# Moving three linear forms of an exponential from VectorE to GpSimd, and converting 67 packs of scores instead of 54

## The chip, the cores and the metric

The kernel runs on one core of one Trainium2 chip. The metric is the device time of one execution in microseconds (us); each version was run several times, and the medians are given. In the first set of runs one execution of the kernel before took 3240 us; it is left out of the ratios, as the fast runs alone count.

The engines are PE (matrix multiply; PEld are its weight loads), DVE (vector), ACT (activation functions), POOL (GpSimd) and SP (here only DMA). The kernel gives each its own stream of instructions in a fixed order, and lets them wait for one another by semaphores. In this kernel the tiles that are named ps_ lie in the memory PSUM, and all of PE's matmuls in the profiles write to them; the others, but for those with dram in their name, lie in the memory SBUF.

## The reference, cut to what matters

Two attention branches over the same input are mixed by a gate. Branch A is ordinary softmax attention with 32 heads of 16 dimensions over 2048 positions, and its exponentials are the bulk of the work:

```python
scores = jnp.einsum("bhqd,bhkd->bhqk", q, k) * (Dh ** -0.5)
p = _softmax(scores, axis=-1)
o = jnp.einsum("bhqk,bhkd->bhqd", p, v)
# ... branch B: linear attention with softmax features (phi); out = g * a + (1 - g) * b
```

## The kernel before

The work of branch A is cut into 32 steps `n` (a quarter of the queries times four heads), each with 16 key blocks `kt` of four score tiles of 128x512. ACT takes the exponential of most tiles, two or three at a time, from a ring of five PSUM banks. Some key blocks per step, called packs here, are taken from ACT: DVE computes their exponential by arithmetic on the bits. A multiplication and addition turn a score into an integer whose high half is the bf16 exponential with a linear mantissa and whose low half is the fraction f; a cubic correction in f is then added. `DVE_COUNT` says how many packs each step has, 54 in all.

```python
DVE_COUNT = (1, 2, 1, 1, 1, 2, 1, 2, ...)           # 54 in all
def dve_pack(self, n, kt, first_pv):
    ...
    for i in range(4):                               # four score tiles of the pack
        m = s.op("pe", ..., matmul(self.bk(b), kT, qT))
        ws.append(s.op("dve", 0.72, EW = tensor_scalar(psum, EC, 127 * 65536, mult, add)))   # int32
    f  = s.op("dve", 1.25, Ef = lo(EW) * 2**-16)     # the low halves as a fraction, f16, 128x2048
    m1 = s.op("dve", 0.71, Em = Ef - 1)
    t  = s.op("dve", 0.71, Et = Ef * (128*EB) + 128*(EA - EB/2))
    u  = s.op("dve", 1.25, Em = Ef * Em)
    g_ = s.op("dve", 1.25, Et = Et * Em)
    for hf in range(2):
        vs.append(s.op("dve", 1.23, ED = EW * 2**-9 + Et))     # uint16 = the bits of bf16
    return s.op("pe", 0.32, four matmuls: ps_ot += Vaug * ED)  # waits for vs
```

The instruction order is not written by hand. A small list scheduler in the kernel is given a planned duration for each operation (the numbers above, in us), priorities and buffer pools; it lays out each engine's program order, and the chip then runs those orders with semaphores. So a duration that is planned too short doesn't make a result wrong. It makes one engine stand, in its order, at something that is not ready, with everything behind it standing too.

The softmax here doesn't subtract the row's maximum and nothing guards it: scores larger than these inputs give would overflow.

## Time and profile before

| | before |
|---|---|
| median time (3 runs; 929.0 with a fourth) | 929.3 us |
| ACT busy | 874.7 us, 94% |
| DVE busy | 753.6 us, 81% |
| PE busy | 785.5 us, 85% |
| POOL busy | 6.6 us, 1% |

The page's first part gives each engine's busy time, share of the span and number of instructions; its second the busy tenths in 40 slices; its fourth the chain of work that ended last.

```profile
span 928.5 us, 12587 instructions
...
PE 785.5 (85%) x5227; PEld 238.8 (26%) x5227; DVE 753.6 (81%) x1062; ACT 874.7 (94%) x801; POOL 6.6 (1%) x10
...
ACT  5998999999999999999999999999999998999995
...
ACT 63%; PE 32%; DVE 2%; SPq 1%; issue 1%; DMA 0%; ACTq 0%
...
```

ACT is at 9 tenths in nearly all slices, and 63% of the chain is ACT's own work, nearly all the rest PE's. In the groups of instructions below, ps_ring is the ring of scores that ACT reads, ps_mp holds the scores of the packs and other products, and ps_ot the sums over the exponentials. A line gives: line, engine, operation, output and inputs, shape, count, busy us and mean ns, and the idle time before them with what ended it.

```profile
...
L590 ACT ACTIVATE ET<-ps_ring 128x1536 bf16<-128x1536 f32 x366 | 533.1, 1457 | 32.2 <-PE ps_ring L574 24.8 <-PE ps_ot L611 5.4
L590 ACT ACTIVATE ET<-ps_ring 128x1024 bf16<-128x1024 f32 x367 | 376.9, 1027 | 3.0 <-PE ps_ring L574 2.5 <-PE ps_ot L611 0.2
...
L645 DVE TENSOR_SCALAR EW<-ps_mp 128x512 int32<-128x512 f32 x216 | 143.4, 681 | 59.7 <-PE ps_mp L641 58.7
L660 DVE SCALAR_TENSOR_TENSOR ED<-EW,Et 128x1024 uint16<-128x1024 int32 x108 | 129.8, 1204 | 0.1
...
L655 DVE TENSOR_TENSOR Em<-Ef,Em 128x2048 f16<-128x2048 f16 x54 | 65.6, 1215 | 0.0
L650 DVE TENSOR_SCALAR Ef<-EW 128x2048 f16<-128x2048 uint16 x54 | 65.5, 1214 | 1.1
L656 DVE TENSOR_TENSOR Et<-Et,Em 128x2048 f16<-128x2048 f16 x54 | 65.3, 1209 | 0.2
...
L796 DVE TENSOR_TENSOR phi<-phi,frec 128x1024 bf16<-128x1024 bf16 x32 | 38.8, 1211 | 0.1
...
L653 DVE TENSOR_SCALAR Et<-Ef 128x2048 f16<-128x2048 f16 x54 | 36.9, 684 | 0.0
...
L668 PE MATMUL ps_ot<-ED,Vaug 128*17 128x512 bf16 x216 | 22.5, 407 | 0.3 <-DVE ED L660 0.3
...
L684 DVE TENSOR_TENSOR T_81<-T_79,rinv 128x256 bf16<-128x256 f32 x32 | 13.2, 413 | 0.1
...
```

A pack costs DVE 4 x 0.68 + 1.21 + 2 x 0.68 + 2 x 1.21 + 2 x 1.20 = 10.1 us. The last line but one (L668) is the matmul that uses a finished pack: PE waited 0.3 us for it in the whole run, so packs were never late. ACT's idle time before its exponentials (32.2 + 3.0 us) is small.

### The profile page before, as it was taken

How to read it: one execution, taken by the hardware profiler on the slowest of the kernel's cores; microseconds unless marked ns; L12 is line 12 of the kernel's file. 1: busy time of each engine (PE TensorE's matmuls, PEld its weight loads, DVE VectorE, ACT ScalarE, POOL GpSimd, SP SyncE). 2: the span in 40 equal slices, each digit the busy share in tenths (PEclk: the TensorE clock that was granted, in tenths of full speed). 3: DMA queues.
4: the chain of work that ended last, by engine and by line, in shares of the span. 5: the costliest groups of instructions: out<-in, count | busy, mean ns of one | idle time of the engine just before them, and what ended most of it. 6: DMA issues, size and time to landing. Idle time of an engine off the chain costs nothing.

```text
span 928.5 us, 12587 instructions
## 1 busy us (share of the span) xinstructions
PE 785.5 (85%) x5227; PEld 238.8 (26%) x5227; DVE 753.6 (81%) x1062; ACT 874.7 (94%) x801; POOL 6.6 (1%) x10
## 2 busy tenths in 40 slices
PE   7989998888888878888888889888787979878795
PEld 2223322222222212222222222222222223222221
DVE  3887787888986887888978786898879798899895
ACT  5998999999999999999999999999999998999995
POOL 2000000000000000000000000000000000000000
PEclk9999999999999999899999999999999799999997
DMA  5131000000000000000000000000000000000000
GB/s 109 52 73 47 1 6 3 1 4 4 4 2 3 4 4 4 4 7 4 9 10 10 4 6 9 9 7 7 1 4 4 4 4 24 4 4 4 4 1 23
DMA packets 25112, 11.18 MB, mean 12 GB/s; under 512 B 18016, under 2 KB 25056, under 8 KB 25056
## 3 DMA queue, kind: packets, MB, share of 16 engines
q1 hardware_dynamic: 23472, 9.99, 4.1%
q8 instruction: 41, 0.67, 0.3%
q10 hardware_dynamic: 1584, 0.39, 0.2%
q14 instruction: 15, 0.12, 0.0%
HBM read 3.16 MB, written 2.10 MB: 6 GB/s over the span
## 4 chain that ended last, share of the span: by engine, by line
ACT 63%; PE 32%; DVE 2%; SPq 1%; issue 1%; DMA 0%; ACTq 0%
ACT ET L590 60%; PE ps_ring L574 15%; PE ps_mp L462 6%; PE ps_ot L611 5%; PE ps_mp L869 3%; ACT phi L790 3%; PE ps_mp L641 2%; SPq L402 1%; DVE EW L645 1%; PE ps_ot L668 1%; PE ps_mp L844 0%; PE ps_mp L809 0%; DMA xT<-in_A_x_dram 0%; DVE fsum L794 0%; DMA out_dram<-outt 0%
## 5 line engine op out<-in xcount | busy, mean ns | idle before, releaser
L590 ACT ACTIVATE ET<-ps_ring 128x1536 bf16<-128x1536 f32 (+1 forms) x733 | 844.7, 1242 | 35.2 <-PE ps_ring L574 27.3
L574 PE MATMUL ps_ring<-qT,kT 64*128 64x512 bf16 (+1 forms) x1832 | 415.8, 399 | 123.6 <-ACT ET L590 118.9
L574 PEld LDWEIGHTS ps_ring<-qT,kT 64*128 64x128 bf16 (+1 forms) x1832 | 105.7, 94 | 426.5 <-ACT ET L590 289.3
L645 DVE TENSOR_SCALAR EW<-ps_mp 128x512 int32<-128x512 f32 x216 | 143.4, 681 | 59.7 <-PE ps_mp L641 58.7
L611 PE MATMUL ps_ot<-ET,Vaug 128*17 128x512 bf16 x1832 | 183.1, 395 | 2.4 <-DVE T_79 L679 1.2
L660 DVE SCALAR_TENSOR_TENSOR ED<-EW,Et 128x1024 uint16<-128x1024 int32 x108 | 129.8, 1204 | 0.1
L641 PE MATMUL ps_mp<-qT,kT 128*128 128x512 bf16 x216 | 81.0, 394 | 3.4 <-DVE EW L645 2.1
L611 PEld LDWEIGHTS ps_ot<-ET,Vaug 128*17 128x17 bf16 x1832 | 43.5, 87 | 109.0 <-issue 100.6
L650 DVE TENSOR_SCALAR Ef<-EW 128x2048 f16<-128x2048 uint16 x54 | 65.5, 1214 | 1.1
L655 DVE TENSOR_TENSOR Em<-Ef,Em 128x2048 f16<-128x2048 f16 x54 | 65.6, 1215 | 0.0
L656 DVE TENSOR_TENSOR Et<-Et,Em 128x2048 f16<-128x2048 f16 x54 | 65.3, 1209 | 0.2
L794 DVE TENSOR_REDUCE fsum<-phi 128x64 f32<-128x1024 bf16 x32 | 38.8, 1213 | 8.5 <-ACT phi L790 8.5
L462 PE MATMUL ps_mp<-xT,WA 128*128 128x512 bf16 x128 | 38.2, 392 | 1.5 <-DMA xT<-in_A_x_dram 1.5
L796 DVE TENSOR_TENSOR phi<-phi,frec 128x1024 bf16<-128x1024 bf16 x32 | 38.8, 1211 | 0.1
L462 PE MATMUL ps_mp<-Wp,xT 128*128 128x512 bf16 x128 | 38.4, 383 | 0.3 <-DVE EW L645 0.3
L652 DVE TENSOR_SCALAR Em<-Ef 128x2048 f16<-128x2048 f16 x54 | 36.7, 680 | 0.7
L653 DVE TENSOR_SCALAR Et<-Ef 128x2048 f16<-128x2048 f16 x54 | 36.9, 684 | 0.0
L679 DVE STREAM_TRANSPOSE T_79<-ps_ot 128x512 f32<-128x512 f32 x32 | 22.9, 715 | 17.2 <-PE ps_ot L611 17.2
L790 ACT ACTIVATE phi<-ps_mp 128x512 bf16<-128x512 f32 x64 | 34.9, 604 | 0.9 <-PE ps_mp L462 0.9
L641 PEld LDWEIGHTS ps_mp<-qT,kT 128*128 128x128 bf16 x216 | 19.7, 97 | 39.5 <-issue 18.3
L519 DVE CAST Vaug<-ps_mp 128x128 bf16<-128x128 f32 (+1 forms) x32 | 13.3, 424 | 13.3 <-PE ps_mp L462 13.2
L869 PE MATMUL ps_mp<-WoA,onT_A 128*128 128x512 bf16 x64 | 20.0, 395 | 3.9 <-DVE onT_A L692 2.3
(66 smaller groups left out, 377.7 us busy)
## 6 DMA issues: line engine op xcount, KB each, us to landing
out_dram<-outt SPq DMA_DIRECT2D x16, 128.0 KB, 1.7
qT<-qst SPq DMA_DIRECT2D x120, 16.0 KB, 1.8
WA<-in_A_wqkv_dram SPq DMA_DIRECT2D x3, 384.0 KB, 4.2
WBV<-in_B_wqkv_dram SPq DMA_DIRECT2D x1, 512.0 KB, 4.5
WoA<-in_A_wo_dram SPq DMA_DIRECT2D x1, 512.0 KB, 3.8
WoB<-in_B_wo_dram SPq DMA_DIRECT2D x1, 512.0 KB, 4.5
WA<-in_A_wqkv_dram ACTq DMA_DIRECT2D x3, 128.0 KB, 3.2
xT<-in_A_x_dram SPq DMA_TRANSPOSE x16, 2.7
```

The lines of the kernel that those rows point to most:

```text
L462: m = s.op("pe", self.c_mm(n), lambda e, c=c: e.matmul(self.bk(b)[:, 0:n], lhs(c), rhs(c), start=(c == 0), stop=(c == 3)), deps if c == 0 ...
L574: return lambda e: e.matmul(self.ps_ring[:, x % RING, :], self.kT[r, g // 2, kt * P:(kt + 1) * P], self.qT[r, n % 2, i, :], start=True, st ...
L590: self.o_exp.append(s.op("act", w * 0.427 + 0.09, lambda e, b0=b0, s0=s0, w=w: e.activation(self.ET[:, s0:s0 + w, :], self.ps_ring[:, b0:b ...
L611: return lambda e: e.matmul(self.ps_ot[32 * i:32 * i + VSL, :], self.Vaug[:, kt, h, :], self.ET[:, (4 * p + k) % NSLOT, :], start=(kt == 0 ...
L641: m = s.op("pe", self.c_mm(512), lambda e, i=i, b=b: e.matmul(self.bk(b), self.kT[:, cp, kt * P:(kt + 1) * P], self.qT[:, n % 2, i, :], st ...
L645: ws.append(s.op("dve", 0.72, lambda e, i=i, b=b: e.tensor_scalar(self.EW[:, ew.idx, i * QCH:(i + 1) * QCH], self.bk(b), float(EC), float( ...
L650: f = s.op("dve", 1.25, lambda e: e.tensor_scalar(self.Ef[:], lo(), float(2.0 ** -16), None, op0=ALU.mult), ws + [self.ed_prev], pr)
L655: u = s.op("dve", 1.25, lambda e: e.tensor_tensor(self.Em[:], self.Ef[:], self.Em[:], ALU.mult), [m1], pr)
L656: g_ = s.op("dve", 1.25, lambda e: e.tensor_tensor(self.Et[:], self.Et[:], self.Em[:], ALU.mult), [t, u], pr)
L660: vs.append(s.op("dve", 1.23, lambda e, c0=c0: e.scalar_tensor_tensor(out=self.ED[:, ed.idx, c0], in0=self.EW[:, ew.idx, c0], scalar=float ...
L790: ex.append(s.op("act", 0.53, lambda e, sg=sg: e.activation(self.phi[:, ph.idx, :, sg, :], self.bk(b).rearrange("p (h f) -> p h f", f=DH), ...
L869: m = s.op("pe", self.c_mm(512), lambda e, src=src, pr=pr, W=W, k=k: e.matmul(self.bk(b), src(), W[:, pr, :], start=(k == 0), stop=(k == l ...
```

## The change

It moves the three linear forms of f (Ef, Em and what was Et) to POOL as multiply-adds straight from the low halves of EW, in halves of 1024 elements. That leaves four big operations of a pack on DVE besides the conversions, and the room is used for more packs. The announcement says 66; the counts add up to 67. Buffers are cut to make space, the copies of K, Q and V get an earlier priority, and the output matmuls wait for all their inputs at the first. A few planned durations of unchanged operations are altered as well (the conversion from 0.72 to 0.67 us, for example).

```diff
-DVE_COUNT = (1, 2, 1, 1, 1, 2, 1, 2, ... 2, 1, 2, 3, 2, 2)
+DVE_COUNT = (1, 2, 2, 2, 2, 2, 2, 2, ... 2, 2, 3, 3, 3, 3)
@@ buffers
-        Ef, Em, Et single; ED 2 buffers; T1, rinv 2; outt 3; phi 6; VB 6
+        Ef, Em 2 buffers; Eg 3 (takes Et's and ED's place); T1, rinv 1; outt 2; phi 5; VB 5
@@ priorities of the copies of Q, K, V: deadline dl
-                         dl - 4 if n0 else dl)
+                         dl - 24 if n0 else dl)
...
@@ dve_pack
-        f = s.op("dve", 1.25, ... tensor_scalar(self.Ef[:], lo(), float(2.0 ** -16), None, op0=ALU.mult), ...)
-        m1 = s.op("dve", 0.71, ... Em = Ef - 1 ...)
-        t = s.op("dve", 0.71, ... Et = Ef * 128*EB + ... )
+        for hf in range(2):
+            c0 = slice(hf * 2 * QCH, (hf + 1) * 2 * QCH)
+            for dst, a1, a0 in forms:                       # Ef, Em, Eg
+                fr.append(s.op("pool", 1.15, lambda e, ...: e.tensor_scalar(
+                    dst()[:, c0], self.EW[:, ew.idx, c0].bitcast(dt.uint16)...[:, :, 0], a1, a0,
+                    op0=ALU.mult, op1=ALU.add), ws[2 * hf:2 * hf + 2], pr))
         u:  Em = Ef * Em      (now waits for the six forms)
         g_: Eg = Eg * Em
         vs: Eg (uint16) = EW * 2**-9 + Eg, in place, two halves
```

More of the change, by code (lines that the diff above doesn't have):

```diff
@@ L32 @@
 EA, EB = 0.34370964, 0.07826797
-DVE_COUNT = (1, 2, 1, 1, 1, 2, 1, 2, 2, 1, 2, 2, 1, 2, 2, 2, 1, 2, 2, 1, 2, 2, 2, 1, 2, 2, 2, 1, 2, 3, 2, 2)
+DVE_COUNT = (1, 2, 2, 2, 2, 2, 2, 2, 2, 2, 2, 2, 2, 2, 2, 2, 2, 2, 2, 2, 2, 2, 2, 2, 2, 2, 2, 2, 3, 3, 3, 3)
 def dve_tiles(n):
@@ L328, in memory @@
         self.EW_p = BufPool(2)
-        at("Ef", [P, 4 * QCH], dt.float16)
-        at("Em", [P, 4 * QCH], dt.float16)
-        at("Et", [P, 4 * QCH], dt.float16)
-        at("ED", [P, 2, 4 * QCH], dt.uint16)
-        self.ED_p = BufPool(2)
-        at("T1", [P, 2, 16, 32], f32)
-        at("rinv", [P, 2, 16], f32)
+        at("Ef", [P, 2, 4 * QCH], dt.float16)
+        at("Em", [P, 2, 4 * QCH], dt.float16)
+        at("Eg", [P, 3, 4 * QCH], dt.float16)
+        self.Eg_p = BufPool(3)
+        at("T1", [P, 16, 32], f32)
+        at("rinv", [P, 16], f32)
         at("T2", [P, 16, 32], bf)
         self.oacc = nc.alloc_sbuf_tensor_at("oacc", [P, 4, D], f32, offset=self.wbt_off)
-        at("outt", [P, 3, D], bf)
-        self.outt_p = BufPool(3)
-        at("phi", [P, 6, H, 2, DH], bf)
-        self.phi_p = BufPool(6)
-        at("VB", [P, 6, 8, 65], bf)
-        self.VB_p = BufPool(6)
+        at("outt", [P, 2, D], bf)
+        self.outt_p = BufPool(2)
+        at("phi", [P, 5, H, 2, DH], bf)
+        self.phi_p = BufPool(5)
+        at("VB", [P, 5, 8, 65], bf)
+        self.VB_p = BufPool(5)
         at("fsum", [P, 2, 64], f32)
@@ L509, in emit_kT @@
         self.o_kT[(cp, j)] = self.evac(b, m, lambda e: e.tensor_copy(
-            self.kT[:, cp, j * QCH:(j + 1) * QCH], self.bk(b)), 512, dl)
+            self.kT[:, cp, j * QCH:(j + 1) * QCH], self.bk(b)), 512, dl - 20 if cp else dl)
     def emit_V(self, t, part):
@@ L520, in emit_V @@
             self.Vaug[:, t, h0:h0 + nh, 0:DH], self.bk(b)[:, 0:n].rearrange("p (h d) -> p h d", d=DH)),
-            n, dl, [self.o_vones])
+            n, dl - 20 if part else dl, [self.o_vones])
     def main_chain(self):
@@ L533, in main_chain @@
             pos.append(pos[-1] + 64 - 4 * len(dve_tiles(n)))
-        self.ed_prev = None
+        self.eq_prev = self.ml_prev = None
         self.units = units
@@ L635, in dve_pack @@
         pr = rel + 12
-        ew, ed = Buf(self.EW_p, 2), Buf(self.ED_p, 1)
+        ew, eg = Buf(self.EW_p, 2), Buf(self.Eg_p, 1)
         ws = []
-        m = None
+        m = self.eq_prev
         for i in range(4):
@@ L642, in dve_pack @@
                 self.bk(b), self.kT[:, cp, kt * P:(kt + 1) * P], self.qT[:, n % 2, i, :], start=True, stop=True),
-                self.o_qT[n] + [self.o_kT[(cp, kt // 4)]], pr, rel, alloc=[b, ew] if i == 0 else [b], cols=512,
+                self.o_qT[n] + [self.o_kT[(cp, kt // 4)]], pr, rel, alloc=[b, ew, eg] if i == 0 else [b], cols=512,
                 order=[m])
-            ws.append(s.op("dve", 0.72, lambda e, i=i, b=b: e.tensor_scalar(
+            ws.append(s.op("dve", 0.67, lambda e, i=i, b=b: e.tensor_scalar(
@@ L646, in dve_pack @@
                 self.EW[:, ew.idx, i * QCH:(i + 1) * QCH], self.bk(b), float(EC), float(127 * 65536),
                 op0=ALU.mult, op1=ALU.add), [m], pr, frees=[b]))
-            self.qk_dve[n] = m
-        lo = lambda: self.EW[:, ew.idx, :].bitcast(dt.uint16).rearrange("p (n two) -> p n two", two=2)[:, :, 0]
-        f = s.op("dve", 1.25, lambda e: e.tensor_scalar(self.Ef[:], lo(), float(2.0 ** -16), None, op0=ALU.mult),
-                 ws + [self.ed_prev], pr)
-        m1 = s.op("dve", 0.71, lambda e: e.tensor_scalar(self.Em[:], self.Ef[:], 1.0, None, op0=ALU.subtract), [f], pr)
@@ L653, in dve_pack @@
-        t = s.op("dve", 0.71, lambda e: e.tensor_scalar(
-            self.Et[:], self.Ef[:], float(128 * EB), float(128 * (EA - EB / 2)), op0=ALU.mult, op1=ALU.add), [f], pr)
-        u = s.op("dve", 1.25, lambda e: e.tensor_tensor(self.Em[:], self.Ef[:], self.Em[:], ALU.mult), [m1], pr)
-        g_ = s.op("dve", 1.25, lambda e: e.tensor_tensor(self.Et[:], self.Et[:], self.Em[:], ALU.mult), [t, u], pr)
+            self.qk_dve[n] = self.eq_prev = m
+        scale = float(2.0 ** -16)
+        forms = ((lambda: self.Ef[:, ew.idx], scale, 0.0), (lambda: self.Em[:, ew.idx], scale, -1.0),
+                 (lambda: self.Eg[:, eg.idx], float(128 * EB) * scale, float(128 * (EA - EB / 2))))
@@ new lines, in dve_pack @@
+        fr = []
+        for hf in range(2):
+            c0 = slice(hf * 2 * QCH, (hf + 1) * 2 * QCH)
+            for dst, a1, a0 in forms:
+                fr.append(s.op("pool", 1.15, lambda e, c0=c0, dst=dst, a1=a1, a0=a0: e.tensor_scalar(
+                    dst()[:, c0], self.EW[:, ew.idx, c0].bitcast(dt.uint16).rearrange(
+                        "p (n two) -> p n two", two=2)[:, :, 0], a1, a0, op0=ALU.mult, op1=ALU.add),
+                    ws[2 * hf:2 * hf + 2], pr))
+        u = s.op("dve", 1.25, lambda e: e.tensor_tensor(
+            self.Em[:, ew.idx], self.Ef[:, ew.idx], self.Em[:, ew.idx], ALU.mult), fr, pr)
@@ L657, in dve_pack @@
+        g_ = s.op("dve", 1.25, lambda e: e.tensor_tensor(
+            self.Eg[:, eg.idx], self.Eg[:, eg.idx], self.Em[:, ew.idx], ALU.mult), [u], pr)
         vs = []
@@ L659, in dve_pack @@
             c0 = slice(hf * 2 * QCH, (hf + 1) * 2 * QCH)
-            vs.append(s.op("dve", 1.23, lambda e, c0=c0: e.scalar_tensor_tensor(
-                out=self.ED[:, ed.idx, c0], in0=self.EW[:, ew.idx, c0], scalar=float(2.0 ** -9), in1=self.Et[:, c0],
-                op0=ALU.mult, op1=ALU.add), [g_], pr, alloc=[ed] if hf == 0 else (), frees=[ew],
-                order=vs[-1:]))
-        self.ed_prev = vs[-1]
+            vs.append(s.op("dve", 1.25, lambda e, c0=c0: e.scalar_tensor_tensor(
+                out=self.Eg[:, eg.idx, c0].bitcast(dt.uint16), in0=self.EW[:, ew.idx, c0], scalar=float(2.0 ** -9),
+                in1=self.Eg[:, eg.idx, c0], op0=ALU.mult, op1=ALU.add), [g_], pr, frees=[ew]))
         def pv(i):
@@ L669, in pv @@
                 self.ps_ot[32 * i:32 * i + VSL, :], self.Vaug[:, kt, h, :],
-                self.ED[:, ed.idx, i * QCH:(i + 1) * QCH].bitcast(dt.bfloat16),
+                self.Eg[:, eg.idx, i * QCH:(i + 1) * QCH].bitcast(dt.bfloat16),
                 start=False, stop=False, tile_position=(0, 32 * i), skip_group_check=True)
         return s.op("pe", 0.32, cols=512, fns=[pv(i) for i in range(4)], deps=vs + [self.o_V[(kt, part)]], prio=pr + 5, order=[first_pv],
-                    frees=[ed])
+                    frees=[eg])
     def norm(self, n, pv):
@@ L679, in norm @@
         tr = s.op("dve", 0.72, lambda e: e.transpose(
-            self.T1[:, j].rearrange("p b s -> p (b s)"), self.ps_ot[:, :]), [pv], prio=-1e4)
+            self.T1[:].rearrange("p b s -> p (b s)"), self.ps_ot[:, :]), [pv, self.ml_prev], prio=-1e4)
         pr = self.tn(n + 1) + 10
-        rc = s.op("dve", 0.25, lambda e: e.reciprocal(self.rinv[:, j, :], self.T1[:, j, :, DH]), [tr], pr)
+        rc = s.op("dve", 0.25, lambda e: e.reciprocal(self.rinv[:], self.T1[:, :, DH]), [tr], pr)
         c0 = DH * (g % 2)
         ml = s.op("dve", 0.40, lambda e: e.tensor_tensor(
-            self.T2[:, :, c0:c0 + DH], self.T1[:, j, :, 0:DH],
-            self.rinv[:, j, :, None].to_broadcast([P, 16, DH]), ALU.mult),
+            self.T2[:, :, c0:c0 + DH], self.T1[:, :, 0:DH], self.rinv[:, :, None].to_broadcast([P, 16, DH]), ALU.mult),
             [rc, self.o_onTA.get((n - 2) // 2) if j == 0 else None], pr)
+        self.ml_prev = ml
         if j == 0:
@@ L793, in feature @@
         flat = lambda: self.phi[:, ph.idx].rearrange("p h s f -> p (h s) f")
-        rd = s.op("dve", 1.24, lambda e: e.tensor_reduce(self.fsum[:, fs.idx, :], flat(), AX.X, ALU.add), ex, r + 10)
+        rd = s.op("dve", 1.22, lambda e: e.tensor_reduce(self.fsum[:, fs.idx, :], flat(), AX.X, ALU.add), ex, r + 10)
         rc = s.op("dve", 0.56, lambda e: e.reciprocal(self.frec[:, fs.idx, :], self.fsum[:, fs.idx, :]), [rd], r + 10)
-        sc = s.op("dve", 1.24, lambda e: e.tensor_tensor(
+        sc = s.op("dve", 1.22, lambda e: e.tensor_tensor(
             flat(), flat(), self.frec[:, fs.idx, :, None].to_broadcast([P, 64, DH]), ALU.mult), [rc], r + 10,
@@ L870, in mms @@
                     self.bk(b), src(), W[:, pr, :], start=(k == 0), stop=(k == len(bl) - 1)),
-                    [dep, self.d_woa, self.d_wob], prio, rel, alloc=[b, *also] if k == 0 else (), order=[m], cols=512,
+                    [x[3] for x in bl] + [self.d_woa, self.d_wob] if k == 0 else (), prio, rel, alloc=[b, *also] if k == 0 else (), order=[m], cols=512,
                     frees=[ba] if ba else ())
```

## The prediction

> **What bounds it now.** The page gives ACT 874.7 us busy of 928.5 (94%), PE 85%, DVE 753.6 (81%), POOL 6.6 (1%). The chain that ended last is 63% ACT and 32% PE. ACT is full between 25 and 910 us: the windows show about 18 us idle in the first 30 us, 10 at the end, some 30 scattered between (58-87 us and 754-783 us are the worst). The waits put most of ACT's idle, 27.3 us in 69 waits, on PE's score matmuls (L574). So ACT's count of exponentials sets the time, and each late DVE result reaches ACT through PE's program order.
>
> **Removed, added, moved.** By the order view the new kernel has 67 packs (268 conversions EW), not 66; before 54. That takes 52 of 1832 tile exponentials from ACT: 844.7/1832 = 0.461 us each, so 24.0 us.
> DVE loses per pack Ef 1.21, Em 0.68, Et 0.68 = 2.58 us (54 x 2.58 = 139 us) and gains 13 packs of 4 x 0.68 + 2 x 1.21 + 2 x 1.20 = 7.55 us (98 us): 713 us.
> POOL gets 402 operations of 128x1024. No record here shows their duration; from its memset of 2048 elements (1.97 us, starts 1.8 apart) I estimate 1.0 to 1.2 us each: 400 to 480 us, half the span.
>
> **Contention.** [...] All four big DVE operations left in a pack (both products, both final combinations) have two SBUF inputs: 67 x 4.83 = 323 us, with the phi scaling some 370. [...] No run here shows the lock yet. In DVE's new order, 118 of those 268 operations stand behind at least two conversions of the next pack, so POOL has work ready there. If each then waits 0.5 to 1 us, DVE loses 60 to 120 us: 770 to 830 of about 905 us, 85 to 92%. That fits, but tightly. It is tightest in the last four steps with three packs each: 3 x 7.55 + 1.4 (normalisation) = 24 us of DVE in a step whose 52 exponentials take 24 us. I expect 5 to 10 us lost there.
>
> **On the critical path.** All 24 us of ACT's saving is, as long as PE isn't held by a late pack. The earlier K, Q, V copies and the output matmuls that wait only at their first should cut a few us of ACT's scattered idle. So 929 - 24 + 7 (tail) - 4 + 1 = 909 us.
>
> **Predicted: 909 us, range 897 to 936; faster by over 2% 0.50, within 2% 0.38, slower 0.12.**
>
> **What shows each step right or wrong.** Page: ACT busy about 850, DVE group EW x268. Groups: the POOL linear forms near 1.1 us; over 1.5 would show POOL too slow or blocked. Groups of Em, Eg products and combinations: 1.21, 1.20 us before; a mean of 1.5 to 2.2 or larger gaps in front of them show the lock, unchanged means show none. Waits: new waits of DVE for POOL, short; ACT's wait for L574's successor should stay below about 35 us. Last-100-us windows: ACT idle above that of before shows the tail lost.
>
> **What would make it wrong.** POOL at 1.6 us or more per form (640 us): packs come late, PE's order holds ACT, time 950 or more. Or DVE waiting in nearly all of the 268 operations. Or no contention at all, and the tail free: 898.

Two sentences are cut under "Contention", because no trace of the kernel before showed what they said: a reason why a reading form on POOL and a DVE operation with two SBUF inputs should hold each other up, and a count that rests on it (440 us of forms and some 370 of such operations, 810 of about 905 us: an estimate from the 1.1 us of a form and the 1.2 us of an operation). The sum to 909 us: 24 us of ACT's saving, 7 lost in the tail, 4 gained by copies and matmuls, 1 for DVE. That each of 118 operations waits 0.5 to 1 us was the author's assumption; the trace after has 0.2 to 0.5 us for one beside a form. "The lock" is the name for this effect, here and below.

## The result, and the profile after

| | before | after |
|---|---|---|
| median time, us | 929.0 (4 runs) | 979.2 (4 runs) |
| ACT busy, us | 874.7 | 856.7 |
| DVE busy, us | 753.6 | 787.7 |
| POOL busy, us | 6.6 | 530.7 |
| mean granted PE clock (share of the full clock, from the trace) | 0.965 | 0.937 |

The changed kernel is slower: 1.054 times the time before, with a 95% interval of 1.051 to 1.058. (Ratios here are the mean time of one kernel's fast runs over that of the other's of the same rounds, so not quite the ratio of the medians.)

The same parts of the page, after:

```profile
span 978.2 us, 12813 instructions
...
PE 784.6 (80%) x5131; PEld 241.7 (25%) x5227; DVE 787.7 (81%) x1004; ACT 856.7 (88%) x780; POOL 530.7 (54%) x412
...
ACT  5997999889999998988999999898898898987781
POOL 2552444554455564545434465266456627778873
...
PE 32%; DVE 26%; ACT 20%; POOL 17%; issue 2%; SPq 1%; DMA 0%; POOLq 0%; another core or an unknown queue 0%; DVEq 0%
...
```

ACT has less to do and is busy for a smaller share (88%). Its part of the chain fell from 63% to 20%; DVE and POOL have 43%, where they had 2%. ACT's slices at the end are 7 and 8 where POOL's are 7 and 8.

The groups after, in the order of those before:

```profile
...
L589 ACT ACTIVATE ET<-ps_ring 128x1536 bf16<-128x1536 f32 x356 | 518.2, 1456 | 79.8 <-PE ps_ring L573 61.3 <-PE ps_ot L610 11.9 <-PE ps_mp L461 1.2
...
L667 DVE SCALAR_TENSOR_TENSOR Eg<-EW,Eg 128x1024 uint16<-128x1024 int32 x134 | 191.1, 1466 | 0.2
L656 POOL TENSOR_SCALAR Em<-EW 128x1024 f16<-128x1024 uint16 x134 | 186.3, 1390 | 0.0
...
L644 DVE TENSOR_SCALAR EW<-ps_mp 128x512 int32<-128x512 f32 x268 | 177.9, 680 | 43.0 <-PE ps_mp L640 38.2 <-PE ps_ot L610 2.6 <-PE ps_ring L573 0.7
...
L662 DVE TENSOR_TENSOR Eg<-Eg,Em 128x2048 f16<-128x2048 f16 x67 | 92.9, 1386 | 0.3
L660 DVE TENSOR_TENSOR Em<-Ef,Em 128x2048 f16<-128x2048 f16 x67 | 86.3, 1288 | 32.2 <-POOL Eg L656 32.0
...
L801 DVE TENSOR_TENSOR phi<-phi,frec 128x1024 bf16<-128x1024 bf16 x32 | 46.9, 1464 | 0.1
...
L673 PE MATMUL ps_ot<-Eg,Vaug 128*17 128x512 bf16 x268 | 28.9, 422 | 42.6 <-DVE Eg L667 41.5 <-issue 0.5 <-DVE onT_A L697 0.5
...
L689 DVE TENSOR_TENSOR T_80<-T_78,rinv 128x256 bf16<-128x256 f32 x32 | 21.6, 676 | 0.3
...
```

The conversions (EW) still take 0.68 us. But the two products went from 1.215 and 1.209 to 1.288 and 1.386 us, the combinations from 1.204 to 1.466, the phi scaling from 1.211 to 1.464, the normalisation from 0.413 to 0.676: all of them DVE operations with two inputs in SBUF, and no other large group. Times their counts (67, 67, 134, 32, 32) that is 68 us. PE now waits 42.6 us at finished packs (0.3 before), and DVE waits 32 us for POOL.

The times of the forms show the same from the other side (shortest, median and longest ns):

```profile
...
L656 POOL TENSOR_SCALAR Ef<-EW x134: 1044/1045/2083, 25.6 to 958.4; 128x1024 f16<-128x1024 uint16 x134
L656 POOL TENSOR_SCALAR Em<-EW x134: 1039/1045/2012, 26.6 to 960.3; 128x1024 f16<-128x1024 uint16 x134
L656 POOL TENSOR_SCALAR Eg<-EW x134: 1044/1045/1897, 27.7 to 961.4; 128x1024 f16<-128x1024 uint16 x134
...
```

A form alone takes 1.045 us, and 126 of the 402 took longer, up to 2.08. What happens there can be watched in one place. First DVE's, then POOL's order of time from 310 to 319 us (start, duration, engine, operation):

```profile
...
310.60 1.69 DVE L660 TENSOR_TENSOR Em<-Ef,Em 128x2048 f16<-128x2048 f16 x1
312.21 0.68 DVE L644 TENSOR_SCALAR EW<-ps_mp 128x512 int32<-128x512 f32 x1
312.81 1.45 DVE L662 TENSOR_TENSOR Eg<-Eg,Em 128x2048 f16<-128x2048 f16 x1
314.19 0.54 DVE L800 RECIPROCAL frec<-fsum 128x64 f32<-128x64 f32 x1
314.65 3.56 DVE L667 SCALAR_TENSOR_TENSOR Eg<-EW,Eg 128x1024 uint16<-128x1024 int32 x2
318.13 2.05 DVE L801 TENSOR_TENSOR phi<-phi,frec 128x1024 bf16<-128x1024 bf16 x1
```

```profile
...
310.17 1.04 POOL L656 TENSOR_SCALAR Ef<-EW 128x1024 f16<-128x1024 uint16 x1 [1.10 <-DVE EW L644]
311.18 2.01 POOL L656 TENSOR_SCALAR Em<-EW 128x1024 f16<-128x1024 uint16 x1
313.27 1.90 POOL L656 TENSOR_SCALAR Eg<-EW 128x1024 f16<-128x1024 uint16 x1
315.25 1.90 POOL L656 TENSOR_SCALAR Ef<-EW 128x1024 f16<-128x1024 uint16 x1
317.11 2.01 POOL L656 TENSOR_SCALAR Em<-EW 128x1024 f16<-128x1024 uint16 x1
```

The first form starts at 310.17 and takes its 1.04 us. DVE's product, started at 310.60, takes 1.69. From there the two engines go in turn: their ends alternate (DVE 312.28, POOL 313.18, DVE 314.25, POOL 315.16, and so on), 0.9 to 1.1 us apart. Each form takes 1.9 to 2.0 us and is followed by the next about 2.0 us later, each two-input operation of DVE takes 1.45 to 2.05 (the line with x2 is one of 1.59 and one of 2.05). DVE's 0.68 us conversion at 312.21 and its 0.54 us reciprocal at 314.19, which have at most one SBUF input, are not slower than before (0.68 and 0.54 us).

Sorting DVE operations of this trace by whether a form was under way at the same time gives the whole picture (counts in brackets):

| DVE operation | no form at the same time, mean us | a form at the same time, mean us |
|---|---|---|
| combination Eg (EW, Eg) | 1.213 (70) | 1.743 (64) |
| first product Em | 1.215 (44) | 1.427 (23) |
| second product Eg | 1.206 (42) | 1.689 (25) |
| phi scaling | 1.213 (17) | 1.749 (15) |
| normalisation T2 | 0.414 (13) | 0.855 (19) |
| conversion EW, from PSUM | 0.681 (104) | 0.679 (164) |
| tensor_reduce fsum, one SBUF input | 1.207 (8) | 1.210 (24) |

So beside a form those with two SBUF inputs stretch by 0.2 us (the first product) to 0.5 us, those with one by nothing. What isn't shown is an operation from SBUF to SBUF with one input that is as fast as the forms on DVE before (0.68 us for 2048 elements): none of that kind is left beside the forms.

Where the time went can be added up. ACT's busy time fell by 18.0 us. After the last exponential 20.3 us pass to the end, 9.5 before: 10.8 us more. Between 25 us and the last exponential ACT's idle time rose by 56.8 us (from 33.0 to 89.8). The sum, -18.0 + 10.8 + 56.8 = 49.6, is the difference of the spans (978.2 - 928.5 = 49.7).

### The profile page after: what moved, and what is told of

The parts are those of the page before. It is cut to its first block, busy times and chain, and to the rows that moved or that the text cites. A ratio compares the mean times of both kernels' runs of the same rounds, so it can differ in the third digit from the quotient of the medians.

```text
span 978.2 us, 12813 instructions
## 1 busy us (share of the span) xinstructions
PE 784.6 (80%) x5131; PEld 241.7 (25%) x5227; DVE 787.7 (81%) x1004; ACT 856.7 (88%) x780; POOL 530.7 (54%) x412
## 4 chain that ended last, share of the span: by engine, by line
PE 32%; DVE 26%; ACT 20%; POOL 17%; issue 2%; SPq 1%; DMA 0%; POOLq 0%; another core or an unknown queue 0%; DVEq 0%
ACT ET L589 19%; PE ps_ring L573 13%; DVE Eg L667 8%; POOL Em L656 6%; PE ps_mp L461 6%; POOL Ef L656 6%; POOL Eg L656 5%; PE ps_ot L610 5%; DVE EW L644 5%; DVE Eg L662 4%; DVE Em L660 3%; PE ps_mp L640 3%; PE ps_mp L874 2%; SPq L401 1%; DVE phi L801 1%
## 5 line engine op out<-in xcount | busy, mean ns | idle before, releaser
L589 ACT ACTIVATE ET<-ps_ring 128x1536 bf16<-128x1536 f32 x712 | 826.6, 1242 | 87.2 <-PE ps_ring L573 67.6
L573 PE MATMUL ps_ring<-qT,kT 64*128 64x512 bf16 (+1 forms) x1726 | 391.5, 405 | 95.3 <-ACT ET L589 88.3
L656 POOL TENSOR_SCALAR Ef<-EW 128x1024 f16<-128x1024 uint16 x134 | 177.3, 1323 | 420.6 <-DVE EW L644 415.3
L644 DVE TENSOR_SCALAR EW<-ps_mp 128x512 int32<-128x512 f32 x268 | 177.9, 680 | 43.0 <-PE ps_mp L640 38.2
L667 DVE SCALAR_TENSOR_TENSOR Eg<-EW,Eg 128x1024 uint16<-128x1024 int32 x134 | 191.1, 1466 | 0.2
L656 POOL TENSOR_SCALAR Em<-EW 128x1024 f16<-128x1024 uint16 x134 | 186.3, 1390 | 0.0
L656 POOL TENSOR_SCALAR Eg<-EW 128x1024 f16<-128x1024 uint16 x134 | 165.1, 1232 | 10.6
L660 DVE TENSOR_TENSOR Em<-Ef,Em 128x2048 f16<-128x2048 f16 x67 | 86.3, 1288 | 32.2 <-POOL Eg L656 32.0
L662 DVE TENSOR_TENSOR Eg<-Eg,Em 128x2048 f16<-128x2048 f16 x67 | 92.9, 1386 | 0.3
L673 PE MATMUL ps_ot<-Eg,Vaug 128*17 128x512 bf16 x268 | 28.9, 422 | 42.6 <-DVE Eg L667 41.5
```

The source lines that it names most:

```text
L573: return lambda e: e.matmul(self.ps_ring[:, x % RING, :], self.kT[r, g // 2, kt * P:(kt + 1) * P], self.qT[r, n % 2, i, :], start=True, st ...
L589: self.o_exp.append(s.op("act", w * 0.427 + 0.09, lambda e, b0=b0, s0=s0, w=w: e.activation(self.ET[:, s0:s0 + w, :], self.ps_ring[:, b0:b ...
L644: ws.append(s.op("dve", 0.67, lambda e, i=i, b=b: e.tensor_scalar(self.EW[:, ew.idx, i * QCH:(i + 1) * QCH], self.bk(b), float(EC), float( ...
L656: fr.append(s.op("pool", 1.15, lambda e, c0=c0, dst=dst, a1=a1, a0=a0: e.tensor_scalar(dst()[:, c0], self.EW[:, ew.idx, c0].bitcast(dt.uin ...
L660: u = s.op("dve", 1.25, lambda e: e.tensor_tensor(self.Em[:, ew.idx], self.Ef[:, ew.idx], self.Em[:, ew.idx], ALU.mult), fr, pr)
L662: g_ = s.op("dve", 1.25, lambda e: e.tensor_tensor(self.Eg[:, eg.idx], self.Eg[:, eg.idx], self.Em[:, ew.idx], ALU.mult), [u], pr)
```

## The experiments

The theories were these. L, the lock: it makes packs late, and PE, in its order, stands at them while ACT runs dry. C, the count: 67 packs through three engines are too many in any case. P and B: the earlier copies, or the smaller buffers, do it. O, the order: the stretch costs only because the plan didn't know it.

### The reads of POOL taken away

```diff
-   e.tensor_scalar(dst()[:, c0], low halves of EW, a1, a0, op0=ALU.mult, op1=ALU.add)
+   e.memset(dst()[:, c0], 32768.0 * a1 + a0)
```

> The changed kernel with each of the 402 linear forms on POOL replaced by a memset of the same 1024 elements to the form's mean value, behind the same waits; nothing else is changed, the instruction order on every engine is the same, and the result is wrong on purpose. POOL then reads no SBUF. If mutual exclusion between POOL's reads and DVE's two-input operations is what makes the packs late (theory L), products and combinations fall from 1.29, 1.39 and 1.47 us back to about 1.21, PE's wait for the combination falls from 41 us to under 10, and the time is 900 to 920 us. If 67 packs are too many for the chain of conversion, POOL and DVE whatever the lock does (theory C), or if the earlier copies displace the packs (theory P), the time stays at 960 or more though the durations shrink.

It took 921.9 us, 0.993 of before (0.987 to 0.9985); it passed the comparison although it is wrong, so that comparison is not a fine test of the exponential. Groups of this run:

```profile
...
L666 DVE SCALAR_TENSOR_TENSOR Eg<-EW,Eg 128x1024 uint16<-128x1024 int32 x134 | 157.2, 1214 | 0.2
L656 POOL MEMSET Eg<- 128x1024 f16 x134 | 127.5, 951 | 0.0
...
L661 DVE TENSOR_TENSOR Eg<-Eg,Em 128x2048 f16<-128x2048 f16 x67 | 81.0, 1209 | 0.3
...
```

The instruction order of every engine is the same as in the changed kernel, POOL is nearly as long in each form (0.951 us), yet no DVE operation stretches: 89 of the 268 products and combinations ran beside a memset for more than 0.1 us and took the same time as the rest (combinations 1.216 us beside one, 1.213 apart). So the reads cost 979.2 - 921.9 = 57 us, and without them the kernel is no slower than before. (That a memset is 0.09 us shorter than a form alone is in these 57 us and wasn't separated.) Theory L holds in this; C and P, which expected 960 us or more, fall.

PE's wait at finished packs fell from 41.5 to 7.8 us, as expected, and DVE's wait for POOL from 32.0 to 4.6. The time is 2 us above the range that was expected (900 to 920), and the gain against before is 7 us, not the 23 that ACT's busy time fell by (852.2 us). ACT's idle in the middle is 10 us more than before, and the stretch after the last exponential 16.8 us instead of 9.5. In that tail the last pack is finished only at 912.5 us, 5.9 us after the last exponential ended (906.6), and PE's matmuls for a later output wait 2.2 us for one of only two output buffers.

### The old count of packs, with and without the reads

> The changed kernel with the pack counts of before (54 packs). ACT has 52 tile exponentials, 24 us, more than in the changed kernel. Theory C: with fewer packs nothing is late, time about 925 to 935 us, faster than the changed kernel by 45 us in spite of ACT's extra work. Theory L: POOL still takes 54 x 6 forms of 1.04 us, DVE's operations still stretch by about 1 us per pack, and part of the loss stays: 935 to 955 us.

> 54 packs as in the run with the counts of before, and POOL's forms replaced by memsets. Theory L: the 27 us that this count lost to before are the lock's, time 915 to 930 us, DVE busy about 615 us. If DVE at 70% still leaves packs late because the chain over three engines is long, 940 us or more.

With the reads 54 packs took 956.2 us (1.029), just above the range of theory L; without, 928.9 (1.000), in the expected range, though DVE was busy for 635 us and not 615. So the lock costs 27 us at 54 packs and 57 us at 67: 24% more packs, which also make the last four steps the fullest, double its price. DVE was busy for only 70% of the run with the reads (669 us), less than before the change, and the kernel was still slower. Theory C's 925 to 935 us was wrong.

### The rest of the change alone

```diff
  (54 packs; the forms back on DVE: Ef 1.21, Em 0.68, Eg 0.68 us; buffers, priorities and gathered waits as changed)
```

> The changed kernel with the three linear forms put back on DVE as before had them (Ef 1.21, Em 0.68, Eg 0.68 us) and the 54 packs of before. What is left of the change is the buffers (five phi and VB, two outt, single T1, double Ef and Em), the priorities and the gathered waits of the output matmuls. If POOL's part is the cause of the loss (theory L), 920 to 935 us, against 956 us of the same with the forms on POOL. If the cut buffers or the new priorities are (theory B), 945 us or more.

It took 928.3 us, 0.999 of before (0.995 to 1.002). The priorities alone, in the kernel before:

> The kernel before with nothing but the earlier priorities of the K, Q and V copies. Theory P (the earlier copies displace pack work on DVE): slower by 1% or more, 940 us or above. Otherwise 920 to 932 us, the same within 1%.

929.7 us, 1.002 (0.996 to 1.007). Neither the buffers nor the priorities cost or bring anything in a kernel without POOL. In the changed kernel the old priorities were tried as well:

> The changed kernel with the old priorities of the K, Q and V copies. Theory L has no stake in them: 970 to 990 us. If the new priorities cost time only where DVE is short of it (theory P in its weaker form), 965 us or less.

It took 995.2 us (1.072), above either range: there the new priorities save 16 us. They were no gain of their own, but they help in this kernel, whose packs are late; why was not followed. Theories P and B fall.

### How the loss grows with the reads

In two runs one or two of the three forms read, and the others are memsets; the order is again the same.

> The changed kernel in which only the first of the three forms reads (Ef), the other two are memsets; same order, result wrong on purpose. [...] If the loss is proportional to the holds: 922 + 57/3 = 941 us. [...]

> The same with two of three forms reading. In proportion: 922 + 57 x 2/3 = 960 us. If steep near saturation (280 + 323 + 52 = 655 us of 930 at two thirds, 795 at three): 935 to 950 us.

Of the first text the case against proportion expected that little is lost, 922 to 932 us. Its sum was of the same kind as the second text's, an estimate from the traces' durations: 140 us for one reading form in each half of a pack, 323 for DVE's products and combinations and 52 for its phi scaling and normalisation, 515 of 930 us.

| forms that read | median us | ratio to before |
|---|---|---|
| 0 | 921.9 | 0.993 |
| 1 | 929.1 | 1.001 |
| 2 | 949.7 | 1.022 |
| 3 | 979.2 | 1.054 |

The steps are 0.8, 2.2 and 3.2% of the time before: the loss is not in proportion to the reads (941 and 960 us were expected then) but grows with each, within the second ranges, which were written down for a loss that gets steep where the busy times of the reading forms and of DVE's two-input operations near the span in sum. Nor is it in proportion to DVE's stretching: against the run without reads DVE is busy for 24, 52 and 68 us longer (744.1, 772.2 and 787.7 against 720.1), and the losses are 7, 28 and 57 us. (Which of the forms reads, the first or a later one, was not varied.)

The last four steps, with three packs each, show this best. Stretches of the changed kernel between the ends of steps, and the same of the run without reads (window, length, then busy us of PE, PEld, DVE, ACT and POOL with the number of instructions, granted PE clock, share of DMA, GB/s):

```profile
...
842.80:871.40 28.60, 20.32 (x128) 5.60 (x128) 26.01 (x27) 23.53 (x21) 20.91 (x14) 0.94 0.01 3
871.40:905.60 34.20, 22.53 (x133) 5.73 (x134) 29.38 (x27) 26.66 (x24) 31.03 (x22) 0.85 0.01 3
905.60:935.90 30.30, 25.85 (x151) 7.22 (x153) 28.11 (x31) 24.67 (x22) 19.46 (x14) 0.95 0.00 1
935.90:968.50 32.60, 17.47 (x112) 4.37 (x113) 25.89 (x27) 19.42 (x18) 25.67 (x18) 0.82 0.00 1
...
```

```profile
...
809.30:832.80 23.50, 19.26 (x128) 5.55 (x130) 20.87 (x27) 23.42 (x21) 11.91 (x14) 1.00 0.01 3
832.80:859.80 27.00, 19.65 (x133) 5.63 (x134) 21.97 (x26) 26.46 (x24) 18.20 (x21) 1.00 0.02 4
859.80:886.80 27.00, 24.36 (x151) 7.17 (x153) 24.50 (x31) 24.17 (x21) 11.61 (x13) 1.00 0.00 1
886.80:913.70 26.90, 16.03 (x112) 4.30 (x113) 21.69 (x26) 19.51 (x18) 15.54 (x18) 0.89 0.00 1
...
```

The four take 125.7 us with the reads and 104.4 without (103.7 before): 21 of the 57 us come from 4 of 32 steps. In turn, a form and a two-input DVE operation take 2.0 us together (the starts at 311.18, 313.27, 315.25). A pack has six of the first and four of the second, ten in all, so as much as five such pairs, and three packs take an estimated 3 x 5 x 2.0 = 30 us of the two engines in turn, against some 24 us of exponentials in a step. The steps took 28.6 to 34.2. In a step of two packs the same estimate is 20 us, of the 29 us that a step took before (929/32).

### Can another order hide it?

```diff
  plan67:    planned durations: form 1.15 -> 1.32, products 1.25 -> 1.29 and 1.39, combination 1.25 -> 1.47, ...
  slack4_67: the PE matmuls of a pack are laid out 4 us after the pack is ready in the plan
  spread67:  -DVE_COUNT = (1, 2 ..., 3, 3, 3, 3)
             +DVE_COUNT = (1, 2 x 10, 3, 3, 2 x 15, 3, 3, 2, 2)
  split512:  forms of 512 elements, 12 in a pack, planned 0.62
```

> The changed kernel with only the planned durations changed, to the means that the changed kernel's trace shows: POOL form 1.32, products 1.29 and 1.39, combination 1.47, phi scaling 1.46, normalisation 0.68 us. The same work in another order. If the stretch costs time only because the order was laid out without it (theory O), PE meets the packs when they are ready: PE's wait for the combination falls below 15 us and the time is 910 to 930 us. If the stretch costs throughput on DVE, or its scatter and not its mean makes packs late, the time stays above 950 us.

> The changed kernel with one difference in its layout: the PE matmuls that consume a finished pack are placed 4 us later in the plan than the plan has the pack ready. Operations, planned durations, lock and counts stay. The lock stretches DVE as before (about 65 us in all). If the time is lost because PE, in program order, stands at a late pack while ACT runs dry (theory L, second half), PE's wait for the combination falls from 41 us to under 15 and the time to 935 to 960 us. If DVE's or POOL's throughput is what is missing, the time stays at 970 or more.

> The changed kernel, 67 packs, with two of the four steps of three packs moved from the last two steps to the middle. Tail term: the last exponential should again end about 10 us before the span's end instead of 20, so 8 to 12 us less than the changed kernel: 965 to 973 us. If the packs in the tail cost nothing of their own, 975 to 985 us.

> The changed kernel with each POOL form cut in two: 12 forms of 512 elements in a pack instead of 6 of 1024, each waiting for one conversion only. A form alone should take about 0.55 to 0.62 us, the total on POOL 10 to 20% more. If the length of one hold is what hurts DVE, its two-input operations stretch by half as much (mean of the combination 1.33 instead of 1.47) and the time falls to 955 to 970 us. If the total held or POOL's own lateness is, since POOL now has to get past DVE twelve times: 980 us or more.

All four were slower than the changed kernel: 994.6 (1.071), 986.3 (1.062), 984.3 (1.059) and 993.4 us (1.069).

The run with 4 us of slack did what was intended at the place it aimed at (the wait was expected to fall under 15 us), and it didn't help: 935 to 960 us were expected. Waits, changed kernel and then this run (who waited for whom: us in total, times, longest):

```profile
...
ACT ET L589 <- PE ps_ring L573: 67.6, 92, 4.3
...
PE ps_ot L673 <- DVE Eg L667: 41.5, 36, 7.6
...
ACT ET L589 <- PE ps_ot L610: 12.6, 12, 3.0
...
```

```profile
...
ACT ET L591 <- PE ps_ring L575: 60.0, 95, 2.4
...
ACT ET L591 <- PE ps_ot L612: 24.5, 18, 4.2
...
PE ps_ot L675 <- DVE Eg L669: 7.4, 1, 7.4
...
```

PE's wait at finished packs fell from 41.5 to 7.4 us, but ACT's waits only moved: from 67.6 + 12.6 to 60.0 + 24.5 us. So the second half of theory L, that PE standing at a late pack is the path by which ACT runs dry, is not confirmed. It isn't refuted either: slack also holds each pack's buffer and the end of its step for longer (ACT's waits for ps_ot doubled), and no run has the slack without the reads. Moving the packs of three removed the tail (10.4 us after the last exponential instead of 20.3), but the moved steps in the middle took 34.8 and 42.8 us. With the measured means in the plan PE waited as long at finished packs as before (41.0 us, where theory O had under 15), and ACT waited 12.4, 5.9 and 8.9 us at the ends of three of the last steps; a mean does not say which operation will be stretched. Forms of half the size stretched the combination to 1.375 us instead of 1.466, but a form alone took 0.618 us, more than half of 1.045, so POOL's busy time rose to 640 us and DVE's wait for POOL from 32 to 75 us. Theory O falls for these layouts. It isn't shown that no layout could hide the lock.

### A version without POOL

Since POOL's reads were the price, the room was sought in DVE's own chain. Replacing the cubic correction by the quadratic f*(f-1)*A drops one form and one product. Its largest relative error, worked out over f from 0 to 1 as |(1 + f + A f (f-1)) / 2^f - 1|, is 0.32% (0.01% for the cubic); rounding to bf16 adds up to 0.39% in either case. That is a small loss of accuracy, not none.

```diff
-  Em = f - 1;  Eg = f * 128*EB + 128*(EA - EB/2);  Em = Ef * Em;  Eg = Eg * Em
+  Em = (f - 1) * 128*EA;  Eg = Ef * Em          # f and both on DVE, none on POOL
```

> A candidate without POOL: the cubic correction of the fraction becomes the quadratic f*(f-1)*A (largest error of the exponential 0.3% instead of 0.01%, below half a unit in the last place of bf16), so a pack costs DVE 4 x 0.68 + 1.21 + 0.68 + 1.21 + 2 x 1.20 = 8.2 us, all of it on DVE; 67 packs, otherwise the changed kernel. DVE busy about 207 + 67 x 8.2 = 757 us, as before. Theory L: without POOL reads no operation stretches, and ACT's saving of 23 us shows but for some 10 us of mid and 7 us of tail that the run without the lock lost: 905 to 925 us. If 67 packs are too many for DVE's order, 930 us or more.

It took 909.8 us, 0.978 of before (0.974 to 0.983). DVE is busy 761 us, ACT 850. Three more of its kind:

> The candidate without POOL, the 67 packs spread as in the run before, and three output buffers instead of two (the room comes from writing f-1 where the product goes). Tail: 16 us between last exponential and end should become 9 to 10, so 900 to 905 us. If the tail isn't set by the packs and the buffers, 907 to 912 us.

> The same with 70 packs: ACT has 12 exponentials, 5.5 us, less; DVE busy about 785 us of 900 (87%). If DVE has the room, 896 to 901 us; if its order is full at 67 packs, 905 us or more.

> The candidate without POOL with 63 packs, two in each step but the first, and three output buffers. ACT has 16 exponentials, 7.4 us, more than with 67 packs. If the steps of three packs cost the candidate what they save, the same as with 67 packs or a little faster: 903 to 910 us. If they paid, 912 to 918 us.

They took 910.6 (0.980), 927.0 (0.998) and 909.6 us (0.980). With 63 packs, two in a step, it is as fast as with 67: the packs that make a third in a step pay nothing, and with 70 packs seven steps of three undo the gain: the time is in the second of the two expected ranges (905 us or more), far above its lower end. In the spread run 900 to 905 us were expected if the tail shrinks. It did (9.6 us instead of 16.2), but ACT's idle in the middle rose by 4.5 us in exchange. The candidate beats both kernels, by about 2% the one before and 7% the changed one; whether it is over or under 2% these rounds don't decide.

## Why the prediction was wrong

- "All 24 us of ACT's saving is [on the critical path], as long as PE isn't held by a late pack": ACT's busy time fell by 22.5 us in the run without reads, 18.0 in the changed kernel. The size was nearly right, but the condition failed: PE waited 42 us at packs, and ACT 67.6 us for its scores, where the prediction had "below about 35".
- POOL: "1.0 to 1.2 us each" was right, 1.045 us alone. The signature named for the lock, stretched products and combinations with gaps before them, was there too, but with means of 1.29 to 1.47 us, below the "1.5 to 2.2" that were written down.
- "DVE loses 60 to 120 us" was right in size: 68 us of stretch and 32 of waiting for POOL. DVE's busy time, 787.7 us, was in the range of 770 to 830. Luck had a part in that: the operations of the packs, which alone were counted, stretched by 51 us, and the phi scaling and the normalisation added 17.
- **"That fits, but tightly" is the step that failed.** It compared DVE's sum with the span (85 to 92%) and let a sum below 100% cost nothing but the "+ 1" in "929 - 24 + 7 (tail) - 4 + 1". The runs show a loss of 57 us by the lock, at a DVE that is busy for 81%, and 27 us at one that is busy for 70%. ACT's idle time in the middle rose by 57 us where the sum had -3. The forms and DVE's two-input operations had been added up too (810 of 905 us), but again as a sum over the run, and such a sum did not tell what a stretch of half a microsecond at a given place does to engines that run in a fixed order with a ring of five banks between PE and ACT. The prediction had named the way into loss, packs that come late so that "PE's order holds ACT, time 950 or more", but expected it only from forms of 1.6 us; their mean was 1.32.
- "I expect 5 to 10 us lost there" (the tail): the last four steps took 125.7 us, 22 more than before, of which 21 are the reads'. The term was too small by half at least, by the estimate above because it counted DVE's 24 us in a step and not the 30 of the two engines in turn.
- "A few us" for the earlier copies: nothing without POOL (1.002), 16 us with it, as a repair.
- Among what would make it wrong, "DVE waiting in nearly all of the 268 operations" was not needed: 112 of the 268 ran beside a form, and all 112 are among the 118 that were counted in the order. 85 of them took over 1.3 us.

What stays open is the exact path by which a stretch reaches ACT in the steps of two packs. PE's stand at the finished pack alone doesn't explain it, since the run that removed most of it moved the wait and gained nothing. PE's granted clock was also lower in the versions with a longer time (0.937, and 0.965 before): between 25 us and the last exponential half clock was granted for 106 us, 58 before and 51 without the reads. Projection matmuls of 512 columns that follow one another start every 0.40 to 0.43 us there (six pairs) and mostly every 0.22 us at full clock, and ACT sat idle for 37% of those 106 us. Whether that is only a consequence of PE's stalls or adds to the loss was not separated.

## What to carry to other kernels

Before work is moved from VectorE to GpSimd, count the VectorE instructions with two SBUF inputs that are left. Here they stretched beside a reading GpSimd instruction (the combination from 1.21 to 1.74 us), and it stretched too (from 1.045 to as much as 2.08): where they went in turn, a pair took 2.0 us, not far below the sum of the two alone (1.04 + 1.21). In the steps where the time of such pairs, by estimate, was over the bottleneck's work (30 us against 24), the step grew to about the sum (28.6 to 34.2 us). Judge by the fullest step and by the order, not by the mean of the run: here the loss was already 3% when VectorE was busy for 70% (54 packs). To prove such an effect, replace the reading instruction by a write-only one of the same length behind the same waits (here a memset of 0.951 us, beside which the combination took 1.216 us and apart from it 1.213); and look first for a shorter formula on the engine that has the work.
